# A Fourier-mixing layer and its feed-forward layer in one kernel: the first phase rebuilt

## The chip, the cores and the metric

The kernel runs on one core of a Trainium2 chip. The metric is the device time of one execution in microseconds (us); lower is better. A core has five engines with queues of their own: PE (TensorE, matrix products; its weight loads are shown as PEld), DVE (VectorE), ACT (ScalarE), POOL (GpSimd) and SP (SyncE, which here only issues transfers). Transfers run on the core's 16 DMA engines; SP, ACT and POOL can issue them.

## The reference

For 8 batches of 3008 tokens of 256 features, a real Fourier transform along the tokens is mixed by a complex 256 x 256 weight, biased, shrunk towards zero by 0.01 and transformed back. A feed-forward layer with a squared ReLU follows.

```
X = rfft(x, axis=1);  Xr, Xi = X.real, X.imag          # x: (8, 3008, 256)
Yr = Xr @ w_r - Xi @ w_i + b_r
Yi = Xr @ w_i + Xi @ w_r + b_i
Y  = sign(Y) * max(|Y| - 0.01, 0)                      # on Yr and Yi apart
y  = irfft(Yr + 1j * Yi, n=3008, axis=1)               # float32
h  = y.reshape(24064, 256) @ moe_w_in                  # 256 -> 2048
out = (max(h, 0) ** 2) @ moe_w_out                     # 2048 -> 256
```

The feed-forward weights come as 64-bit floats (two 32-bit words each).

## The kernel before

**Tiling.** A token index is split as 3008 = 47 x 64, so that the transform takes two stages of matrix products. The host folds the 47 rows into 24 pairs and lays x out as 120 rows (24 pairs x 5) by 13 blocks, each block two planes of 256 numbers a row. Stage one (`Fwd32` for batch 0, `Fwd2` for batch 1, `Fwd` after) adds and subtracts the two planes of a block, multiplies by the constant `am32` and stores the result (`xe`) to an intermediate `s1` in device memory. Stage two of batch 0 is made of 24 units (`Unit32`, one for each pair index g): it reads its rows of `s1` (`ka`), multiplies by a constant of its own (`kbb`: `fwd`), copies the spectrum to SBUF (`kx`: `bins`), multiplies by the mix weights (`w32`: `mix`), adds the bias and shrinks (`kv`: `shrink`), multiplies back (`kk`: `back`) and stores the result to `s3` as a high half (`kuh`) and a low half (`kul`), both in fp32r, a 32-bit format that PE multiplies in one pass where float32 takes two (`store_back`). The other batches do the same in pairs (`Pair`) with fp32r products.

**Phases.** The first phase (its own memory pool, `FRONT` gives the number of buffers for each name) does stage one of batch 0, all its units, and the first seven blocks (`PRE`) of stage one of batch 1. `ring` holds the seven `Fwd32` (two blocks each but the last); four of their x buffers (`big`) exist. Between the units stand the conversions of the feed-forward weights: 16 parts of 512 KB (`moe_part`, loaded into `dst`) are turned from 64-bit floats into fp32r halves by `convert` (`bits`, `join`, then `split` or, for w_in, `win_sums`), mostly DVE work. Two parts are converted ahead of the units, eight between them, two straight after, and four later. The seven blocks of batch 1 (`second[q].run`) are multiplied after the last unit, with the sum and difference made by PE (`am32`, `nam`, its negative), copied by ACT to an `xf` buffer, of which there are three, and stored over POOL's queue.

The main loop then walks over 48 tiles of 8 steps (`Step`): the second half of the way back (`Back`, reading `s3` into `du`, copied by ACT as `dy`), the split of the tokens into halves (`Tokens`), and the feed-forward products (`psh`, `pso`), with the remaining stage-one blocks and the pairs of the next batches hung between the steps at written times (`jobs`). Weight parts 13, 14 and 15 are converted at slots 1, 3 and 5 (`LATER`).

**Order.** A tile framework orders each engine's queue by program order and a simulated time line. `tc.issue_after(x)` puts what follows behind x on its queue; every queue runs strictly in order, so a waiting instruction holds all behind it. Buffers of one name are used in turn: a new one waits until the last reader of the old one, a transfer too, has ended.

In the unit loop, round r issues `fwd` and `bins` of unit r + 1, `shrink` of r - 1, `back` and `store` of r - 2 and `mix` of r. PE thus sees forward product, back product, mix product. `store_back` has two ways to the low half: for units 0 to 21 ACT writes a second copy `ku` of the product, and POOL subtracts (22 times); for the last two DVE subtracts straight from PSUM. PSUM has eight banks of 2 KB a partition; the first phase uses six (`psf`).

## Time and profile before

| what | us |
|---|---|
| median of three runs | 2613.54 (2612.62 to 2613.75) |
| span of the profiled execution, first to last instruction | 2611.6 |
| PE busy | 2565.9 (98%) |
| DVE, ACT, POOL busy | 1788.3, 1672.8, 1658.6 |
| DMA moved | 250.51 MB, mean 96 GB/s |
| first product of a unit starts | 34.40 |
| last unit's back product starts | 109.75 |

The profile is that of one execution; its own time is its span and what lies around it, and the span is 1.9 us under the median of the runs. A row of instructions reads: start in us, length, engine, line of the code, operation, what it writes and reads, shapes, and in brackets how long the engine stood idle before it and what ended that. A row of a group gives the count, the busy time, the mean of one in ns, and the idle time before. A row of waits reads: who waited for whom, us in total, times, the longest. A row of transfers gives the queue, the count, KB of one and the median us from issue to landing. On PE one float32 product is two instructions, and a busy PE isn't PE at its peak. Lengths overlap by somewhat less than 0.1 us on DVE and ACT, so the distance between starts is the better measure in a full queue.

### The profile page before, as it was taken

The page shows a single profiled execution, that of the slowest core. Times are in us where ns is not written, and L with a number is a line of the kernel's source. Part 1 is how long each engine was busy: PE and PEld are TensorE (multiplying, and loading weights), DVE is VectorE, ACT ScalarE, POOL GpSimd, SP SyncE. Part 2 cuts the span into 40 slices and gives each one's busy share as a digit, 9 for nine tenths or more (in the row PEclk, how much of TensorE's full clock was granted, in tenths as well). Part 3 has the DMA queues.
Part 4 walks back from the last instruction along what each step waited for, and adds up shares of the span by engine and source line. Part 5 has one row for each costly group of instructions (what it writes and reads, how often), then busy time and mean ns, then how long its engine had stood idle before and what let it go on. Part 6 is the DMA issues. An engine that isn't in the chain of part 4 may idle for free.

```text
span 2611.6 us, 47553 instructions
## 1 busy us (share of the span) xinstructions
PE 2565.9 (98%) x16908; PEld 2347.7 (90%) x16908; DVE 1788.3 (68%) x3797; ACT 1672.8 (64%) x2434; POOL 1658.6 (64%) x1635
## 2 busy tenths in 40 slices
PE   6899999999999999999999999999999999999999
PEld 4789989999999999999999999999999999999998
DVE  7787766667767767577676776667676677765554
ACT  3566656666666666666666666666666666666665
POOL 2256666666766667667666676666667666666564
PEclk8999999999999999999999999999999999999999
DMA  8733332333332333233332333323332223221100
GB/s 265 253 100 106 102 113 80 96 108 104 94 94 78 113 104 88 82 95 114 103 92 82 97 110 100 100 76 100 104 106 82 69 81 101 72 65 40 34 17 17
DMA packets 191070, 250.51 MB, mean 96 GB/s; under 512 B 21790, under 2 KB 135958, under 8 KB 190834
## 3 DMA queue, kind: packets, MB, share of 16 engines
q1 hardware_dynamic: 177970, 223.40, 28.1%
q0 software_dynamic: 12864, 24.07, 3.9%
q8 instruction: 136, 2.23, 0.4%
q14 instruction: 100, 0.82, 0.1%
HBM read 146.85 MB, written 100.53 MB: 95 GB/s over the span
## 4 chain that ended last, share of the span: by engine, by line
PE 93%; DVE 3%; DMA 2%; POOL 1%; issue 1%; ACT 0%; SPq 0%; POOLq 0%; ACTq 0%; DVEq 0%
PE pso L484 39%; PE psh L484 35%; PE psf L301 7%; PE psf L280 3%; PE psf L236 2%; PE psf L333 2%; PE psf L464 1%; PE psf L465 1%; PE psf L461 1%; DMA du<-s 1%; DMA s<-xe 1%; PE psf L415 1%; PE psf L352 0%; DVE kv L101 0%; PE psf L373 0%
## 5 line engine op out<-in xcount | busy, mean ns | idle before, releaser
L101 POOL TENSOR_TENSOR mg<-mc,mg 128x500 fp32r<-128x500 f32 (+1 forms) x768 | 974.8, 1290 | 594.6 <-ACT mg L97 562.0
L484 PE MATMUL pso<-mg,wout 128*128 128x500 f32 (+1 forms) x4608 | 1176.2, 392 | 1.5 <-ACT mg L97 1.3
L484 PE MATMUL psh<-yt,win 128*128 128x250 f32 (+1 forms) x8064 | 1070.1, 281 | 1.6 <-DVE yr L471 1.0
L484 ACT ACTIVATE mc<-mc 128x1000 f32<-128x1000 f32 (+1 forms) x768 | 802.7, 1045 | 414.7 <-DVE mc L484 405.9
L484 PEld LDWEIGHTS psh<-yt,win 128*128 128x128 f32 x8064 | 1020.5, 189 | 33.9 <-PE psh L484 2.0
L484 PEld LDWEIGHTS pso<-mg,wout 128*128 128x128 f32 x4608 | 818.6, 189 | 130.0 <-POOL mg L101 2.0
L484 DVE TENSOR_TENSOR mc<-psh,mv 128x500 f32<-128x500 f32 (+3 forms) x768 | 419.6, 548 | 432.2 <-PE psh L484 399.7
L97 ACT CAST mg<-mc 128x1000 fp32r<-128x1000 f32 (+1 forms) x384 | 397.0, 1034 | 18.3
L484 DVE TENSOR_TENSOR mv<-psh,mu 128x500 f32<-128x500 f32 (+1 forms) x384 | 260.8, 679 | 55.3 <-PE psh L484 22.4
L301 PE MATMUL psf<-wx,kxh 128*128 128x256 f32 x1008 | 207.2, 282 | 1.6 <-ACT xe L97 0.7
L98 DVE COPY mp<-psh 128x250 f32<-128x250 f32 (+1 forms) x384 | 159.9, 416 | 32.5 <-PE psh L484 8.9
L101 POOL TENSOR_TENSOR ksl<-kv,ksh 128x512 fp32r<-128x512 f32 x84 | 108.7, 1294 | 100.6 <-ACT ksh L97 100.5
L301 PEld LDWEIGHTS psf<-wx,kxh 128*128 128x128 f32 x1008 | 166.6, 189 | 6.3 <-ACT xe L97 0.9
L484 DVE TENSOR_TENSOR mu<-psh,mp 128x250 f32<-128x250 f32 (+1 forms) x384 | 160.7, 418 | 11.5
L484 DVE TENSOR_TENSOR mc<-psh,mp 128x250 f32<-128x250 f32 (+1 forms) x384 | 157.1, 409 | 5.8 <-PE psh L484 4.2
L215 POOL TENSOR_TENSOR xs<-xt 120x256 f32<-120x256 f32 x156 | 114.9, 757 | 67.3 <-DMA xt<-x_in 66.6
L322 DVE TENSOR_TENSOR kv<-psf,ke 64x256 f32<-64x256 f32 x336 | 141.8, 422 | 18.1 <-PE psf L301 10.0
L301 PE MATMUL psf<-wx,kxl 128*128 128x256 f32 x504 | 141.5, 281 | 3.6 <-DVE kxl L101 3.6
L97 ACT COPY dy<-psf 128x188 f32<-128x188 f32 x256 | 77.0, 313 | 83.6 <-PE psf L465 82.7
L97 ACT CAST ksh<-kv 128x512 fp32r<-128x512 f32 x84 | 52.1, 620 | 118.0 <-DVE kv L101 117.2
L313 DVE TENSOR_TENSOR ke<-psf,bias 128x512 f32<-128x512 f32 x84 | 58.1, 691 | 100.6 <-PE psf L301 100.2
L97 ACT CAST kuh<-psf 128x256 fp32r<-128x256 f32 x192 | 68.3, 372 | 87.8 <-PE psf L333 72.5
(103 smaller groups left out, 2575.0 us busy)
## 6 DMA issues: line engine op xcount, KB each, us to landing
du<-s SPq DMA_DIRECT2D x128, 256.0 KB, 2.8
s<-kuh SPq DMA_DIRECT2D x192, 128.0 KB, 1.8
s<-kul SPq DMA_DIRECT2D x192, 128.0 KB, 2.0
ka<-s SPq DMA_DIRECT2D x84, 256.0 KB, 3.4
kcm<-cm_in POOLq DMA_DIRECT2D x84, 256.0 KB, 3.3
s<-xe SPq DMA_DIRECT2D x85, 240.0 KB, 2.4
xt<-x_in SPq DMA_DIRECT2D x84, 240.0 KB, 3.4
du<-s SPq DMA_DIRECT2D x256, 64.0 KB, 2.8
```

Source lines behind the costliest of these rows:

```text
L97: return act.copy(out=out, in_=in_)
L98: return eng.tensor_copy(out=out, in_=in_)
L101: return eng.tensor_tensor(out=out, in0=a, in1=b, op=ALU.subtract)
L215: return eng.tensor_tensor(out=out[:, :n], in0=self.xt[:, :n, 0], in1=self.xt[:, :n, 1], op=(ALU.add, ALU.subtract)[t])
L236: nc.tensor.matmul(ps[:M1, t], am32[:, t], self.u[:, t], start=True, stop=True)
L280: nc.tensor.matmul(pv[:, :, c, g, :], self.a[:, g, c * 128:(c + 1) * 128], bg, start=True, stop=True)
L301: self.last = nc.tensor.matmul(ps, l, wx[j][:, k, c, :], start=n == 0, stop=n == 5)
L313: dve.tensor_add(out=self.e, in0=self.pe, in1=bias)
L322: dve.tensor_add(out=v[64 * r:64 * r + 64, g], in0=ps[gs], in1=self.e[gs, r])
L333: nc.tensor.matmul(ps[:, :D], self.cm[:, g, j * 128:(j + 1) * 128], r[:, g], start=n == 0, stop=n == 2)
L415: nc.tensor.matmul(ps[:, :D], self.x[:, c, js], w32[j][:, c], start=n == 0, stop=n == 3)
L484: last_of[eng] = op(*args, **kwargs)
```

## The change

The change touches the first phase only, and what it hands on.

- x is laid out on 128 rows (the last eight are zeros) and `Fwd32` loads all of them. Both folds are made by DVE (one was POOL's), both copies out of PSUM by ACT (one was DVE's).
- The queue of ACT issues `am32`, the mix weights, the bias and the first group of unit constants; the bias arrives as four rows in a block of 34 and is added by one more product in `mix` (fp32r, high and low half against a selector `sel`) in place of DVE's addition of `b32`.
- `shrink` becomes one ReLU on ACT and one DVE operation, min(y + 0.01, relu(y - 0.01)). DVE makes every low half (`kul`) from PSUM; POOL and `ku` drop out of the units.
- Units load two at a time (`ka`, four pairs of buffers in place of five single ones). The constants `kbb` and `kk` of a group of four units are loaded behind the store of unit 3, 7, 11 and 15 (groups 2 to 5); groups 0 and 1 ahead.
- The weight parts are loaded behind the first unit loads (three of them) and then behind the store of every second unit; ten conversions instead of eight stand between the units, none ahead. The bias for the later batches follows unit 2's store.
- Three blocks of batch 1 (`FILL`) are loaded during stage one and multiplied straight after it, seven more (3 to 9) after the last unit, so that `PRE` is 10 instead of 7 and three instead of six are left for the main loop. `xf` has two buffers instead of three, `psf` eight instead of six.

```diff
 FRONT = {
-    "a32": 1, "b32": 1, "w320": 1, "w321": 1, "big": 4, "small": 4, "ds": 1, "dw": 3, "ka": 5, "xe": 7,
-    "kv": 3, "psf": 6, "x6": 7, "xf": 3, "nam": 1,
+    "w320": 1, "w321": 1, "big": 4, "small": 4, "ds": 1, "dw": 3, "ka": 4, "xe": 7, "sel": 1, "bb": 1,
+    "kv": 3, "psf": 8, "x6": 7, "xf": 2, "nam": 1,
 }
...
-    nc.sync.dma_start(am32, a32)
     w32 = []
...
-
     def load_mix_weights():
-        b32 = T("b32", [128, D], F32)
-        for j, v in enumerate((b_r, b_i)):
-            with tc.issue_after(ring[3].folds[1].ins):
-                pool.dma_start(b32[64 * j:64 * j + 64, :], v.unsqueeze(0).broadcast_to([64, D]))
         for j, w in enumerate((w_r, w_i)):
...
             w32.append(st)
-            nc.sync.dma_start(st, w.rearrange("(c p) d -> p c d", p=128))
+            act.dma_start(st, w.rearrange("(c p) d -> p c d", p=128))
+
+    def split_mix_weights():
         wd = T("wd", [128, 2, D], F32, tag="small")
...
             sub(dve, wx[1][:, j], w, wx[0][:, j])
-        return b32
+
+    def load_bias():
+        bf = T("bf", [34, D], F32, tag="small")
+        sf = T("sf", [34, 128], F32, tag="small")
+        act.dma_start(bf, b2)
+        act.dma_start(sf, sel)
+        bb = T("bb", [34, D], F32R)
+        one = T("sel", [34, 128], F32R)
+        copy(act, one, sf)
+        copy(act, bb, bf)
+        sub(dve, bb[32:], bf[32:], bb[32:])
+        return one, bb
...
-        def join(self):
+        def join(self, after=None):
             self.w = w = T("dw", [128, 512], F32)
-            dve.scalar_tensor_tensor(
-                out=w, in0=self.st[:, :, 0].bitcast(U32), scalar=2.0 ** -52, in1=self.a,
-                op0=ALU.mult, op1=ALU.mult,
-            )
+            with tc.issue_after(after.cut.ins) if after else nullcontext():
+                dve.scalar_tensor_tensor(
+                    out=w, in0=self.st[:, :, 0].bitcast(U32), scalar=2.0 ** -52, in1=self.a,
+                    op0=ALU.mult, op1=ALU.mult,
+                )
             dve.tensor_add(out=w, in0=w, in1=self.f.bitcast(F32))
...
         for v, m in ((uh, 4 * g), (ul, 128 + 4 * g if 4 * g < 64 else 32 + 4 * g)):
-            nc.sync.dma_start(rows[m * NP:m * NP + 128], v.bitcast(F32))
-        return done
+            put = nc.sync.dma_start(rows[m * NP:m * NP + 128], v.bitcast(F32))
+        return done, put
...
         def load(self):
-            self.xt = T("x4", [M1, 2, 2, D], F32, tag="big")
+            self.xt = T("x4", [128, 2, 2, D], F32, tag="big")
             self.get = nc.sync.dma_start(self.xt[:, :self.n], x[self.b, :, self.q:self.q + self.n])
...
             n = self.n
-            self.ps, self.folds = [], []
-            for t, eng in enumerate((dve, pool)):
+            self.ps = []
+            for t in range(2):
                 u = T("x2", [M1, 2, D], F32, tag="small")
-                self.folds.append(self.fold(eng, u, t))
+                self.cut = dve.tensor_tensor(
+                    out=u[:, :n], in0=self.xt[:M1, :n, 0], in1=self.xt[:M1, :n, 1], op=(ALU.add, ALU.subtract)[t]
+                )
                 ps = bank([128, 2, D])
...
         def put(self):
+            n = self.n
             self.ev = T("xe", [M1, 2, 2, D], F32)
             for t, ps in enumerate(self.ps):
-                self.done = copy((act, dve)[t], self.ev[:, :self.n, t], ps[:M1, :self.n])
+                self.done = copy(act, self.ev[:, :n, t], ps[:M1, :n])
             self.last = self.store()
...
-    kk = [None, None]
+    group = {}
+
+    def load_group(k, after, eng=nc.sync):
+        group[k] = []
+        for name, src in (("kbb", bm), ("kk", c32)):
+            t = T(name, [128, 4, 128], F32)
+            with tc.issue_after(after.ins):
+                after = eng.dma_start(t, src[:, 4 * k:4 * k + 4])
+            group[k].append(t)
+        return after
...
         def load(self):
-            self.a = T("ka", [128, D], F32)
-            self.get = nc.sync.dma_start(self.a, s1[self.b][self.g, :N1].rearrange("n t c -> (n t) c"))
-            if self.g % 4 == 0:
-                with tc.issue_after(units[self.g - 4].get.ins if self.g else ring[2].last.ins):
-                    for j, (name, src) in enumerate((("kbb", bm), ("kk", c32))):
-                        kk[j] = T(name, [128, 4, 128], F32)
-                        nc.sync.dma_start(kk[j], src[:, self.g:self.g + 4])
-            self.m, self.k = kk[0][:, self.g % 4], kk[1][:, self.g % 4]
+            if self.g % 2 == 0:
+                self.pair = T("ka", [128, 2, D], F32)
+                self.get = nc.sync.dma_start(
+                    self.pair, s1[self.b][self.g:self.g + 2, :N1].rearrange("g n t c -> (n t) g c")
+                )
+            else:
+                self.pair = units[self.g - 1].pair
+            self.a = self.pair[:, self.g % 2]
...
                 nc.tensor.matmul(
-                    ps[:, c, 0:128], self.a[:, c * 128:(c + 1) * 128], self.m, start=True, stop=True
+                    ps[:, c, 0:128], self.a[:, c * 128:(c + 1) * 128], group[self.g // 4][0][:, self.g % 4], start=True, stop=True
                 )
...
             self.ps = ps = bank([128, 512])
+            nc.tensor.matmul(ps[:, :D], one, bb, start=True, stop=False)
             for n in range(4):
...
                 js = slice(64, 192) if j == 0 else slice(0, 128)
-                nc.tensor.matmul(ps[:, :D], self.x[:, c, js], w32[j][:, c], start=n == 0, stop=n == 3)
+                nc.tensor.matmul(ps[:, :D], self.x[:, c, js], w32[j][:, c], start=False, stop=n == 3)
...
             self.v = v = T("kv", [128, D], F32)
-            cl = T("kc", [128, D], F32)
-            dve.tensor_add(out=v, in0=self.ps[:, :D], in1=b32)
-            dve.tensor_scalar(out=cl, in0=v, scalar1=-LAM, scalar2=LAM, op0=ALU.max, op1=ALU.min)
-            self.cut = sub(dve, v, v, cl)
+            r = T("kr", [128, D], F32)
+            act.activation(r, self.ps[:, :D], AF.Relu, bias=low)
+            self.cut = dve.scalar_tensor_tensor(
+                out=v, in0=self.ps[:, :D], scalar=LAM, in1=r, op0=ALU.add, op1=ALU.min
+            )
...
             self.ps = ps = bank([128, 512])
-            nc.tensor.matmul(ps[:, :D], self.k, self.v, start=True, stop=True)
+            nc.tensor.matmul(ps[:, :D], group[self.g // 4][1][:, self.g % 4], self.v, start=True, stop=True)
...
         def store(self):
-            self.done = store_back(self.b, self.g, self.ps[:, :D], pool if self.g < G - 2 else None)
+            self.done, self.put = store_back(self.b, self.g, self.ps[:, :D], None)
...
     parts = [moe_part(q) for q in (0, 1, 8, 9, 2, 3, 10, 11, 4, 5, 12, 13, 6, 7, 14, 15)]
-
+    PRE, FILL = 10, 3
+    second = [Fwd2(1, q) for q in range(J)]
+
+    act.dma_start(am32, a32)
+    dve.memset(low, -LAM)
     for f in ring[:FRONT["big"]]:
         f.load()
+    nam = T("nam", [M1, M1], F32)
+    act.mul(nam, am32[:, 1], -1.0)
+    one, bb = load_bias()
     for r in range(len(ring) + 1):
...
         at(ring, r - 1, "put")
-    with tc.issue_after(ring[2].last.ins):
-        b32 = load_mix_weights()
-
-
-    EARLY, LATE = 2, 6
+        if r == 1:
+            with tc.issue_after(ring[0].done.ins):
+                load_mix_weights()
+                load_group(0, ring[0].done, act)
+        if r == 4:
+            for q in range(FILL):
+                second[q].load_early(ring[2].last)
+    for q in range(FILL):
+        second[q].run()
+    for u in units[:4]:
+        u.load()
+    last = load_group(1, units[0].get)
+    with tc.issue_after(ring[-1].done.ins), tc.issue_after(ring[-1].cut.ins):
+        split_mix_weights()
+
+    AHEAD, LATE = 3, 6
     LATER = {1: 13, 3: 14, 5: 15}
...
-    def convert(n, after=None):
+    def convert(n, after=None, then=None):
         p = parts[n]
         p.bits(after)
-        p.join()
+        p.join(then)
         if n % 4 > 1:
...
-    last = ring[1].last
-    for p in parts[:EARLY]:
+    for p in parts[:AHEAD]:
         with tc.issue_after(last.ins):
...
         last = p.get
-    for n in range(EARLY):
-        convert(n)
-    paced = [(n, 2 * (n - EARLY)) for n in range(EARLY, len(parts) - LATE)]
-    loads = [(k - 1, parts[n]) for n, k in paced] + [(20 + j, p) for j, p in enumerate(parts[-LATE:-2])]
-
-    PRE = 7
-    nam = T("nam", [M1, M1], F32)
-    act.mul(nam, am32[:, 1], -1.0)
-    second = [Fwd2(1, q) for q in range(J)]
-    for r in range(-5, len(units) + 3):
+    loads = parts[AHEAD:-2]
+    for r in range(-1, len(units) + 3):
         at(units, r + 5, "load")
...
         at(units, r, "mix")
-        if r == 4:
-            with tc.issue_after(units[8].get.ins):
-                for j, v in enumerate((b_r, b_i)):
-                    nc.sync.dma_start(bias[:, j, :], v.unsqueeze(0).broadcast_to([128, D]))
-                last_pool = pool.dma_start(dx_sb, dx)
-        while loads and loads[0][0] <= r:
-            p = loads.pop(0)[1]
-            with tc.issue_after((units[r + 5] if r + 5 < len(units) else units[-1]).get.ins):
-                p.load()
-        for n, k in paced:
-            if k + 3 == r:
-                convert(n, units[k])
-        if 0 <= r - 12 < PRE:
-            second[r - 12].load_early(units[min(r + 5, len(units) - 1)].get)
-    for q in range(PRE):
+        k = r - 2
+        if k == 2:
+            with tc.issue_after(units[k].put.ins):
+                for j in range(2):
+                    nc.sync.dma_start(bias[:, j, :], b2[j:j + 1].broadcast_to([128, D]))
+            last_pool = pool.dma_start(dx_sb, dx)
+        if k >= 3 and k % 4 == 3 and k // 4 + 2 < G // 4:
+            load_group(k // 4 + 2, units[k].put)
+        n, odd = divmod(k, 2)
+        if k >= 0 and not odd and n < len(parts) - LATE:
+            convert(n, units[k], units[k])
+            if loads:
+                with tc.issue_after(units[k].put.ins):
+                    loads.pop(0).load()
+        if k >= 12 and k - 12 + FILL < PRE:
+            second[k - 12 + FILL].load_early(units[k].put)
+    for p in loads:
+        with tc.issue_after(units[-1].put.ins):
+            p.load()
+    for q in range(FILL, PRE):
         second[q].run()
-    chain[nc.sync], chain[pool] = units[-1].get, last_pool
+    chain[nc.sync], chain[pool] = units[-1].put, last_pool
     front.close()
...
     xp = xp.reshape(B, N2, R, J, D)
-    xi = np.zeros((B, G, R, J, 2, D), x.dtype)
-    xi[:, :, :, :, 0] = xp[:, :G]
-    xi[:, 1:, :, :, 1] = xp[:, :G - 1:-1]
+    xi = np.zeros((B, 128, J, 2, D), x.dtype)
+    xv = xi[:, :M1].reshape(B, G, R, J, 2, D)
+    xv[:, :, :, :, 0] = xp[:, :G]
+    xv[:, 1:, :, :, 1] = xp[:, :G - 1:-1]
+    xi[:, :M1] = xv.reshape(B, M1, J, 2, D)
     am, bm, cm, dm = _consts()
+    b2, sel = np.zeros((34, D), x.dtype), np.zeros((34, 128), x.dtype)
+    for j, v in enumerate((b_r, b_i)):
+        b2[j] = b2[32 + j] = v
+        sel[j::32, 64 * j:64 * j + 64] = 1
     arrays = {
-        "x_in": xi.reshape(B, M1, J, 2, D),
-        "w_r_in": w_r, "w_i_in": w_i, "b_r_in": b_r, "b_i_in": b_i,
+        "x_in": xi,
+        "w_r_in": w_r, "w_i_in": w_i, "b2_in": b2,
         "w_in_in": moe_w_in.view(np.int64), "w_out_in": moe_w_out.view(np.int64),
...
         "c32_in": cm.transpose(1, 0, 2).astype(np.float32),
+        "sel_in": sel,
     }
```

## Prediction before the run

> **What bounds the kernel now.** I read the page's head, then a table of the span cut at the seams of the stages (columns: stretch in us, its length, busy time of PE, PEld, DVE, ACT and POOL with instruction counts, granted clock, DMA share, GB/s).
>
> ```profile
> span 2611.6 us, 47553 instructions
> 0.00:34.40 34.40, 14.72 (x29) 6.01 (x29) 19.64 (x33) 8.97 (x15) 11.89 (x14) 0.89 0.86 268
> 34.40:110.26 75.86, 68.69 (x337) 59.73 (x337) 67.18 (x146) 39.42 (x113) 20.66 (x22) 0.96 0.84 259
> 110.26:139.06 28.80, 24.82 (x118) 20.99 (x117) 19.20 (x46) 13.09 (x28) 4.08 (x8) 0.88 0.67 212
> 139.06:170.00 30.94, 29.33 (x184) 26.27 (x183) 30.58 (x59) 20.90 (x31) 14.27 (x12) 1.00 0.39 111
> 170.00:2611.60 2441.60, 2428.31 (x16247) 2234.70 (x16245) 1651.69 (x3519) 1590.44 (x2248) 1607.68 (x1580) 1.00 0.30 87
> ```
>
> From 170 us on PE is busy 2428.3 of 2441.6 us and the change moves nothing there. The prize lies in the first 139 us: stage one with its loads (0 to 34.4), the 24 units (34.4 to 110.3), seven blocks of the second batch and the way into the main loop (110.3 to 139.1). Behind these, 139 to 170 is odd: DVE is busy 30.58 of 30.94 us, PE 29.33, so both are full.
>
> How the first stretch ends, by the chain that ended last (start, length, what) and the DMA columns of 1 us windows:
>
> ```profile
> 1.27 4.89 DMA x<-x_in
> 6.18 0.70 DVE x L215
> 6.93 9.34 PE psf L373 x14
> 24.57 7.54 DMA s<-xe
> 32.25 2.05 DMA ka<-s
> 34.40 2.04 PE psf L401 x8
> ...
> 10.00:11.00 1.00, 1.00 (x2) 0.32 (x1) 0.01 (x1) 0.00 (x0) 0.71 (x1) 1.00 0.96 238
> 17.00:18.00 1.00, 1.00 (x4) 0.50 (x3) 1.00 (x1) 0.00 (x0) 1.00 (x2) 1.00 1.01 391
> 24.00:25.00 1.00, 0.00 (x0) 0.00 (x0) 0.00 (x0) 0.48 (x1) 0.00 (x0) 1.00 1.03 415
> 30.00:31.00 1.00, 0.00 (x0) 0.00 (x0) 1.00 (x3) 0.00 (x0) 0.00 (x0) 0.50 0.32 125
> ```
>
> The unit loads wait for the last store of stage one. It is issued at 24.57 and needs 7.54 us because the queue ahead of it holds weights; DMA moves 415 GB/s then and falls off only at 30. While nothing but x, on 120 rows, is in flight (10 to 11) the share is as full, 0.96, at 238 GB/s; with 128-row weights mixed in it is 391.
>
> **The change part by part.**
>
> *Stage one.* x comes as 6.5 loads of 128 x 4 KB (0.524 MB; 3.41 MB in all, before 3.12). I take 390 GB/s from the 17 to 18 row, since that is what 128-row traffic reaches; the other bound is the 238 of the 10 to 11 row. At 390 the first block needs 1.35 us instead of 2, am32 and dx_sb no longer go ahead of it, and it is issued about 0.5 us sooner: PE starts near 5.0 instead of 6.93. Both folds on DVE cost 2 x 0.7 a block, less than PE needs for it. PE's pitch sets the rest (weight loads of one stream, start and length):
>
> ```profile
> 10.49 0.32 PEld L373 LDWEIGHTS psf<-x,am 120*120 120x120 f32 x1 [0.53 <-issue]
> 11.35 0.32 PEld L373 LDWEIGHTS psf<-x,am 120*120 120x120 f32 x1 [0.53 <-issue]
> ...
> 13.52 0.18 PEld L373 LDWEIGHTS psf<-x,am 120*120 120x120 f32 x1 [0.24 <-issue]
> 13.95 0.18 PEld L373 LDWEIGHTS psf<-x,am 120*120 120x120 f32 x1 [0.25 <-issue]
> ```
>
> 0.86 us an instruction until about 13, 0.43 after: slow for the first 6.1 us of work. With that kept, two blocks in the slow 6.1 us and then 4.5 at 4 x 0.43, PE ends near 5.0 + 6.1 + 8 = 19 (before 6.93 + 14.72 = 21.65 at the earliest), and the last store is issued near 20. What must be moved ahead of the unit loads: x 3.41, stores 3.12, mix weights and first group 1.05, three blocks of the second batch 0.74, am32 0.12: 8.44 MB, and 0.2 to 0.5 of the POOL queue's stores between. From 1.8 us at 390 GB/s that ends at 1.8 + 8.44/0.39 = 23.5; if the last 1.3 to 1.7 MB, all on 120 rows, go at 240, at 26 or 27. Taking 25.5 and half a us for landing, the unit loads go out at 26 and, with the 2.05 + 0.1 of the chain, PE starts the units at 28.2 instead of 34.4: **-6 us** (bounds -2.5, x at 238; -8). Seven DMA issues and both evictions move to ACT, beside PE's 1.72 us a block; if ACT is late, eight PSUM banks hold four blocks, and behind them PE would wait for it.
>
> A rule that speaks against this: the Trainium skill, "DMA: Bandwidth & Descriptors", section "Why a DMA increments its semaphore by 16 and not by 1", says a transfer runs on the largest number of engines up to 16 that divides its row counts. By it 120 rows use 15 engines and 128 use 16, which would be only a sixteenth more rate, an estimate of 254 GB/s, and as x also has a fifteenth more bytes, no gain. The row at 17 to 18 speaks for more, but it is a mixture; so this is a rival below.
>
> *The units.* DVE loses the add, clip and subtract and gains one two-input operation and POOL's low half; POOL is idle. Groups of DVE from 43 to 98 us (busy us, mean ns), and DVE's own low half:
>
> ```profile
> L101 DVE TENSOR_TENSOR kv<-kv,kc 128x256 f32<-128x256 f32 x18 | 9.6, 532 | 0.0
> L420 DVE TENSOR_TENSOR kv<-psf,b 128x256 f32<-128x256 f32 x18 | 7.4, 413 | 1.0 <-PE psf L415 1.0
> L421 DVE TENSOR_SCALAR kc<-kv 128x256 f32<-128x256 f32 x18 | 6.7, 372 | 0.1
> 109.91 0.42 DVE L101 TENSOR_TENSOR kul<-psf,kuh 128x256 fp32r<-128x256 f32 x1 [0.30 <-issue]
> ```
>
> 1.32 us a unit becomes 2 x 0.42 = 0.84, 24 x 0.48 = 11.5 us of DVE. But two more conversions come in from the wait before the units. The stage's DVE time without the 24 x 1.32 of the units is 67.18 - 31.7 = 35.5 for eight of them, 4.4 each; so DVE keeps 67.2 - 11.5 + 8.9 = 65 us, and PE becomes the bound. PE's own pace, where DVE had slack:
>
> ```profile
> 101.70 1.89 PE L415 MATMUL psf<-w,kx 128*128 128x256 f32 x8
> 103.43 0.61 PE L401 MATMUL psf<-kbb,ka 128*128 128x128 f32 x4
> 103.87 0.60 PE L426 MATMUL psf<-kv,kk 128*128 128x256 f32 x2
> 104.31 1.89 PE L415 MATMUL psf<-w,kx 128*128 128x256 f32 x8
> ...
> 139.06 2.62 PE L484 MATMUL psh<-yt,win 128*128 128x252 f32 x21
> ```
>
> 104.31 - 101.70 = 2.61 a unit, and the bias product is one more of the 0.12 kind (2.62/21): 2.73. Then 24 x 2.73 = 65.5, plus 3 for the slow clock at the start, 2 for the first unit's chain and 1.5 for the last: 72 us at best against 75.86. Two new waits eat into it:
>
> ```profile
> POOL kul L101 <- DMA s<-kul: 26.3, 8, 4.5
> ...
> s<-kul SPq DMA_DIRECT2D x24, 128.0 KB, 3.9
> kbb<-bm_in SPq DMA_DIRECT2D x4, 256.0 KB, 3.6
> ...
> 109.75 0.67 PE L426 MATMUL psf<-kv,kk 128*128 128x256 f32 x2 [0.97 <-DVE kv L101]
> 111.40 0.38 SPq L255 DMA_DIRECT2D s<-kul  x1
> ```
>
> First, a group of constants is now issued only after the store of unit 3, 7, 11 or 15 and needed by the forward product two units on. Back product to its store's issue is 111.40 - 109.75 = 1.65, with busy engines about 2.1; 0.4 to issue, 3.6 to land: 6.1, against PE's two units less one forward product, 2 x 2.73 - 0.44 = 5.0. PE stalls about 1.1, four times: 4 us if DVE and ACT use none of it, 0 if a load is quicker. Second, POOL waited eight times for one of the two low-half buffers; the same wait now stands in DVE's queue, ahead of the next shrink, which PE's back product awaits. A store of 3.9 us fits into two units (5.5), one of the longer ones does not; I take 1. ACT's relu replaces its plain copy and costs nothing while ACT has half its time free. I put the stage at 74.4: **-1.5 us** (bounds -4 and +12, below).
>
> *The seven later blocks.* As many as before, but through two output buffers instead of three.
>
> ```profile
> ACT xe L97 <- DMA s<-xe: 5.7, 3, 2.0
> s<-xe POOLq DMA_DIRECT2D x7, 240.0 KB, 5.3
> ...
> 123.98 0.59 ACT L97 COPY xe<-psf 120x512 f32<-120x512 f32 x1 [2.02 <-DMA s<-xe]
> 124.67 0.53 ACT L97 COPY dy<-psf 128x188 f32<-128x188 f32 x2
> ```
>
> ACT already waits 5.7 us for the buffers and the first dy copy stands behind the last block. With two, a copy and its store, 0.6 + 0.3 + 5.3, pass two blocks: 3.1 us a block against 1.73 of PE, up to 5 x 1.37 = 7 us more before dy. Part is idle time that another wait would fill, since the first full step of the main loop starts only at 139, and dy copies may be ordered between: **+2.5 us** (0 to +7). One weight part more goes out just before the du loads (0.5 MB, 1.3 us), inside this.
>
> *The main loop.* Three blocks fewer.
>
> ```profile
> 141.52 1.46 PE L352 MATMUL psf<-xt,am 120*120 120x256 f32 x6
> 142.82 0.59 PE L352 MATMUL psf<-xt,nam 120*120 120x256 f32 x2
> ```
>
> 143.25 - 141.52 = 1.73 us of PE each (the next block starts at 143.25), 5.2 for three. They run instead while PE waits for stage one's stores, from about 19 to 24, which costs nothing there as long as they end before 28. In the main loop the two blocks that come first stand where PE waits anyway, and the others in the stretch where DVE is full (30.58 of 30.94): a shorter PE queue there waits for DVE. So of the 5.2 I count **-2 us** (0 to -5.2).
>
> Sum: -6 - 1.5 + 2.5 - 2 = -7. The span of the profiled execution, 2611.6, becomes 2604.6; the median of the runs, 2613.54, lies 1.9 above that span, for what stands around it. Forecast: **2606.5 us**.
>
> **The rivals.**
>
> *All of it lands (2598 us).* Units at PE's pace (-4), DVE with slack while it converts so that all three blocks count (-5.2), the tail's two buffers covered (0): -6 - 4 - 5.2 = -15.2. For it: PE ran at 2.61 a unit when it could. Against: DVE's full stretch behind 139.
>
> *x is not faster (2610).* If 128 rows move x at the 238 GB/s that 120 rows reach, it takes 3.41/0.238 = 14.3 us instead of 8.7, and PE waits for blocks. The stage's gain falls from 6 to 2.5, the sum to -3.5. For it: the DMA share is as full at 238 as at 391. Against: both rows are of the same core and the same kind of load. The rule of the Trainium skill's page above comes near to this case; that 15 of 16 engines would give 238 beside 391 it does not explain.
>
> *The tail takes it back (2614.5).* Two buffers cost the full 7, the units gain nothing (0), DVE eats the three blocks (0): -6 + 7 = +1. It is the buffers' landing that decides, from 5 us on.
>
> *The low half's wait stops DVE (2620.5), the slower one.* If the 26.3 us that POOL waited move to DVE whole, DVE has 65 + 26 = 91 us, less some 3 that the missing POOL no longer stretches (the subtract's 532 ns beside 413): 88, and the stage becomes 12 longer than 75.86: -6 + 12 + 2.5 - 2 = +6.5. For it: eight of 22 stores were late for two buffers, and weights now stand straight behind every second store. Against: POOL was itself held by ACT and stood in a chain with SP, and DVE's low half comes earlier. It decides once most stores take longer than two units, 5.5 us, to land.
>
> **How the numbers follow.** My forecast 0.40, all lands 0.22, x not faster 0.15, the tail 0.13, DVE stopped 0.10. A measurement of this kernel tells about 0.2%, 5.2 us, from no change: faster is below 2608.3, slower above 2618.7. The forecast's own terms spread by 4 us or so, so 0.29 of its 0.40 counts as faster, 0.11 as the same; all lands is faster whole; of x not faster 0.03 is faster; the tail is the same, 0.01 of it slower; DVE stopped is slower by 0.09. Faster 0.54, same 0.36, slower 0.10. The range leaves out the lower part of the second case and most of the last: 2596 to 2616.
>
> **What would show it.** Right: the x-only windows at 350 GB/s or more; unit loads issued by 27; first unit product by 29; back products 2.7 to 3.1 us apart, with short waits of PE for kbb at units 8, 12, 16, 20; DVE's waits for the kul stores a few us in all; ACT's waits for the output buffers 10 us or more ahead of the first dy; in the main loop three blocks fewer and PE with more gaps between its first steps. Wrong: x at 240 to 260 GB/s; last store of stage one landing after 30; the distance from the first unit product to the last back product over 80 us, or under 71; the first steps of the main loop full again more than 10 us earlier, or later, than 139 us. The forecast also fails if the new order moves a stall inside the main loop, which I took as unchanged.

## The result, and the profile after

The changed kernel took 2629.50 us in the median of three runs (2623.79 to 2630.95; a fourth, at 13598.11, lay far above all others and is left out), beside 2613.64 for the kernel before, run together with it: a ratio of 1.0057 (1.0041 to 1.0073). It is slower by 0.57%, where 2606.5 was forecast, and lies outside the range of 2596 to 2616. Its profiled execution has a span of 2629.2 us (time 2630.95), 17.6 more than the 2611.6 of before.

The span of the changed kernel, cut at five events: the first product of a unit, the last back product, the first full step of the main loop (the first `psh` group of 15 or more products), the first outputs of a tile (ACT's first `mo`), the end. Columns as in the prediction's first table. Behind it the two rows of the kernel before that the prediction's table cuts elsewhere.

```profile
0.00:33.89 33.89, 21.86 (x52) 10.99 (x53) 12.02 (x21) 12.77 (x24) 2.52 (x8) 0.95 0.83 282
33.89:116.79 82.90, 78.71 (x358) 60.44 (x358) 60.06 (x132) 43.56 (x118) 0.00 (x0) 0.96 0.78 245
116.79:147.72 30.93, 23.09 (x97) 19.04 (x97) 15.65 (x38) 11.73 (x25) 4.06 (x8) 0.83 0.59 188
147.72:215.39 67.67, 58.33 (x371) 52.85 (x372) 58.00 (x106) 41.07 (x59) 39.87 (x36) 0.92 0.26 75
215.39:2629.20 2413.81, 2401.01 (x16056) 2208.93 (x16054) 1631.59 (x3478) 1570.11 (x2221) 1584.12 (x1556) 1.00 0.29 87
```

```profile
134.49:198.50 64.01, 61.02 (x392) 54.92 (x391) 54.07 (x107) 42.62 (x62) 36.81 (x36) 1.00 0.36 101
198.50:2611.60 2413.10, 2400.15 (x16064) 2209.17 (x16062) 1632.56 (x3478) 1570.02 (x2221) 1585.14 (x1556) 1.00 0.30 87
```

The last row is the same in both within 0.7 us: all that changed lies before the first tile outputs. The same cut for every kernel of this study (lengths of the stretches; runs are told of below):

| kernel | first unit product | units | to first full step | to first tile outputs | rest | span |
|---|---|---|---|---|---|---|
| before | 34.40 | 75.35 | 24.74 | 64.01 | 2413.1 | 2611.6 |
| after | 33.89 | 82.90 | 30.93 | 67.67 | 2413.8 | 2629.2 |
| e1_bias128 | 32.56 | 78.61 | 30.6 | 68.0 | 2409.7 | 2619.5 |
| e2_biasf32 | 32.10 | 82.75 | 31.6 | 66.9 | 2414.3 | 2627.7 |
| e3_xf3 | 32.61 | 82.83 | 31.9 | 68.4 | 2412.4 | 2628.1 |
| e4_biaslate | 31.14 | 85.18 | 31.7 | 67.8 | 2413.7 | 2629.5 |
| e5_kbbearly | 32.12 | 76.69 | 31.0 | 68.9 | 2415.0 | 2623.6 |
| e6_nofill | 30.66 | 81.22 | 31.3 | 64.6 | 2413.3 | 2621.0 |
| e8_later | 33.20 | 82.79 | 31.0 | 60.0 | 2422.0 | 2629.0 |
| e9_pre7 | 32.23 | 81.58 | 22.5 | 64.4 | 2415.8 | 2616.5 |
| c1 | 31.25 | 69.97 | 22.5 | 64.2 | 2413.7 | 2601.6 |
| c4 | 28.02 | 67.48 | 24.8 | 64.9 | 2412.7 | 2597.9 |

After less before, with the forecast's term: start -0.5 (-6), units +7.6 (-1.5), to the first full step +6.2 (+2.5), to the first tile +3.7 (-2), rest +0.7. Six kernels whose stage one is as the change has it, but for the shape or format of the bias block (e1, e2, e3, e5, e8, e9), start between 32.1 and 33.2, so the start varies by 1 us or more from run to run, and a fair term for it is -0.5 to -2.3. Each row is one execution; e1's is that of its fastest run (2621.26 us, median 2626.65).

### The profile page after: what moved, and what is told of

Same layout as the page of the kernel before. It is cut to its first block, busy times and chain, and to the rows that moved or that the text cites. A ratio compares the mean times of both kernels' runs of the same rounds, so it can differ in the third digit from the quotient of the medians.

```text
span 2629.2 us, 47506 instructions
## 1 busy us (share of the span) xinstructions
PE 2583.0 (98%) x16932; PEld 2352.2 (89%) x16932; DVE 1777.3 (68%) x3773; ACT 1679.2 (64%) x2445; POOL 1630.6 (62%) x1607
## 4 chain that ended last, share of the span: by engine, by line
PE 93%; DMA 3%; DVE 2%; POOL 1%; issue 1%; ACT 0%; SPq 0%; ACTq 0%; POOLq 0%; DVEq 0%
PE pso L507 39%; PE psh L507 35%; PE psf L310 7%; PE psf L289 3%; PE psf L245 2%; PE psf L342 2%; PE psf L437 1%; PE psf L487 1%; PE psf L488 1%; PE psf L484 1%; DMA du<-s 1%; DMA s<-xe 1%; DMA kbb<-bm_in 1%; PE psf L422 0%; DMA sf<-sel_in 0%
## 5 line engine op out<-in xcount | busy, mean ns | idle before, releaser
L494 DVE TENSOR_TENSOR yr<-psf,dy 128x188 f32<-128x188 f32 (+4 forms) x256 | 78.2, 313 | 68.1 <-ACT dy L98 61.6
```

What stands on the lines that cost most here:

```text
L494: self.cut = dve.tensor_add(out=o, in0=ps[:, 0, lo:hi], in1=y[:, c, lo:hi])
```

## The experiments

Two theories of the loss were set against each other first: that the units got longer because the bias product costs much more than its size says (A), or because loads come too late for them (B: `kbb`, or a stop of DVE behind the low half's stores); then the start, the way into the main loop and the main loop were tried one at a time. The time of each kernel is a median, and the ratio behind it is to the kernel before, run together with it. By these ratios e1 to e5 and e8 can't be told from the changed kernel: their intervals overlap its 1.0041 to 1.0073. Only e6, e9, c1 and c4 lie below it. What is said of the others rests on the stretches of one execution each.

### e1 and e2: the shape of the bias product

One unit of the changed kernel in PE's timeline (start, length, line, operation, count):

```profile
64.32 1.99 PE L437 MATMUL psf<-w,kx 128*128 128x256 f32 x8
66.15 0.61 PE L422 MATMUL psf<-kbb,ka 128*128 128x128 f32 x4
66.59 0.60 PE L449 MATMUL psf<-kv,kk 128*128 128x256 f32 x2
67.12 0.38 PE L433 MATMUL psf<-bb,sel 34*128 34x256 f32 x1
67.43 1.99 PE L437 MATMUL psf<-w,kx 128*128 128x256 f32 x8
```

67.43 - 64.32 = 3.11 us a unit, where before it was 2.61. The new row itself takes 67.43 - 67.12 = 0.31, the back product ahead of it 0.53 (0.44 before), and the mix behind it 1.83 instead of 1.73. PE's weight loads show the seam:

```profile
66.48 0.30 PEld L449 LDWEIGHTS psf<-kv,kk 128*128 128x128 f32 x2
67.12 0.18 PEld L433 LDWEIGHTS psf<-bb,sel 34*128 34x128 f32 x1 [0.33 <-issue]
67.43 1.59 PEld L437 LDWEIGHTS psf<-w,kx 128*128 128x128 f32 x8
```

The load of the 34-row weights starts at 67.12, with its product and not under the one before it; the unit's own loads (66.48) run ahead of their products (66.59). e1 puts the same bias into 128 rows, 94 of them zero; e2 keeps 34 rows and makes them plain float32.

```diff
-        bb = T("bb", [34, D], F32R)
-        one = T("sel", [34, 128], F32R)
-        copy(act, one, sf)
-        copy(act, bb, bf)
+        bb = T("bb", [128, D], F32R)             # e1; e2: [34, ...] in F32
+        one = T("sel", [128, 128], F32R)
+        pool.memset(bb.bitcast(F32), 0.0)        # and one
+        copy(act, one[:34], sf)
+        copy(act, bb[:34], bf)
...
```

> The changed kernel with one edit: the bias product has 128 rows (34 as before, the rest zeros) instead of 34, still fp32r; nothing else. In the changed kernel a unit takes PE 3.11 us from mix product to mix product: bias 0.31, mix 1.92, forward 0.44, back 0.43, where the mix took 1.73 before. Theory A, the 34-row shape is what PE pays for when it stands between 128-row products: bias falls to about 0.12 and mix to 1.73, a unit to about 2.73, 24 units 9 us shorter unless DVE or the waits for kbb take it back. Theory B, PE pays for each change between fp32r and float32: the unit stays at 3.1 us.

> The changed kernel with one edit: the bias product keeps its 34 rows but is float32 (two passes). Theory B (change of format): bias 0.43 and mix back to 1.73, a unit about 3.03 us, 2 us less over 24. Theory A (shape of 34 rows): the mix keeps its 1.92, the bias takes about 0.6, a unit about 3.4, 7 us more over 24.

e1: 2626.65 us, a ratio of 1.0053 (1.0035 to 1.0070) to before. A unit of it, in the same view:

```profile
56.36 0.60 PE L451 MATMUL psf<-kv,kk 128*128 128x256 f32 x2
56.60 0.47 PE L435 MATMUL psf<-bb,sel 128*128 128x256 f32 x1
56.91 1.89 PE L439 MATMUL psf<-w,kx 128*128 128x256 f32 x8
58.63 0.61 PE L424 MATMUL psf<-kbb,ka 128*128 128x128 f32 x4
59.08 0.60 PE L451 MATMUL psf<-kv,kk 128*128 128x256 f32 x2
```

59.08 - 56.36 = 2.72 us a unit, 0.39 less with more rows to multiply: 9.4 us over 24 units. e2 (2630.03 us, 1.0073, 1.0056 to 1.0090) has 3.43 a unit, 0.32 more than after, for a second instruction of the same shape (0.70 for the two). Its 24 units still take 82.75 us and not 7 more: no wait for `kbb` is left in them, and the granted clock was 1.00 from their start. So it is the shape between products of 128 rows that costs, and not a change between fp32r and float32: theory A. The Trainium skill, "TensorEngine Tiling (Array Packing)", section "Tiling Modes", says that a change of the array's tiling mode drains TensorE, and that there are modes of 64 and of 32 rows. The weight load that no longer overlaps and the two stretched neighbours fit that; no row shows the mode itself.

Of the 9.4 us only 4.3 came through in e1's units (78.61). And 2.1 of the 4.3 lie ahead of the first back product (7.32 us beside 9.47), where the granted clock was at 0.50 for 3.4 us in e1 and for 6.8 in the changed kernel, which the edit doesn't reach. Behind it PE's busy time falls by 6.9 us (62.37 beside 69.24), but PE, now ahead, waits 4.6 longer for `kbb`, so that 2.1 are left (waits of PE over the units, in us, times, longest; the changed kernel first, then e1):

```profile
PE psf L422 <- DMA kbb<-bm_in: 3.5, 3, 1.5
```

```profile
PE psf L424 <- DMA kbb<-bm_in: 8.1, 4, 3.5
```

### e5: the constants earlier

```diff
...
-        if k >= 3 and k % 4 == 3 and k // 4 + 2 < G // 4:
-            load_group(k // 4 + 2, units[k].put)
+        if k >= 3 and k % 4 == 3 and k // 4 + 2 < G // 4:
+            load_group(k // 4 + 2, units[k].put, names=("kk",))
+        if k >= 1 and k % 4 == 1 and k // 4 + 2 < G // 4:
+            load_group(k // 4 + 2, units[k].put, names=("kbb",))
```

> The changed kernel with one edit: a group's forward constants kbb are loaded behind the store of units 1, 5, 9, 13 instead of 3, 7, 11, 15 (their buffer is free from then); kk stays. In the changed kernel PE waits for kbb before units 8, 16 and 20, 1.1, 1.0 and 1.5 us by the profile and 3.9 us by the starts of its products. Theory: the waits go and the 24 units take 79 us instead of 82.9. Rival: the wait is lent time, DVE and the stores catch up in it, and PE waits elsewhere; the stage stays over 82.

2625.66 us, 1.0052 (1.0036 to 1.0068). No wait for `kbb` is left. The units take 76.69 instead of 82.90, of which two stretches (first product to first back product, then to the last) show what is the edit's, after first and e5 second:

```profile
33.89:43.36 9.47, 9.47 (x34) 7.55 (x35) 0.52 (x2) 1.96 (x7) 0.00 (x0) 0.64 0.98 343
43.36:116.79 73.43, 69.24 (x325) 52.88 (x324) 59.54 (x131) 41.60 (x111) 0.00 (x0) 1.00 0.75 233
```

```profile
32.12:38.46 6.34, 6.34 (x35) 5.27 (x35) 0.42 (x1) 2.13 (x8) 0.53 (x1) 1.00 0.97 286
38.46:108.81 70.35, 68.51 (x325) 53.19 (x324) 59.73 (x131) 41.58 (x111) 0.00 (x0) 1.00 0.84 264
```

3.1 us lie behind the first back product, which is about the wait of 3.5; the other 3.1 lie before it, where PE's granted clock was 0.64 in the one execution and 1.00 in the other. The edit doesn't reach that stretch, so that half is not its gain, and the edit's own is close to the 79 us expected (82.90 - 3.1 = 79.8). What set the clock there isn't settled; PE had stood idle 2.16 us before its first unit product in the one and 0.46 in the other.

### e4 and e6: the start

The load of the selector in the chain of the changed kernel (start, length), ACT's queue, and four windows of 1 us (the last column GB/s):

```profile
1.70 9.83 DMA sf<-sel_in
...
9.44 0.40 ACT L98 CAST bb<-bf 34x256 fp32r<-34x256 f32 x1 [4.06 <-DMA bf<-b_in]
9.75 0.57 ACT L98 COPY xe<-psf 120x512 f32<-120x512 f32 x1
11.56 0.30 ACT L98 CAST sel<-sf 34x128 fp32r<-34x128 f32 x1 [1.24 <-DMA sf<-sel_in]
11.76 0.57 ACT L98 COPY xe<-psf 120x512 f32<-120x512 f32 x1
...
8.00:9.00 1.00, 1.00 (x2) 0.28 (x1) 0.40 (x1) 0.00 (x0) 0.00 (x0) 1.00 1.08 372
10.00:11.00 1.00, 1.00 (x2) 0.00 (x0) 0.97 (x2) 0.32 (x1) 0.00 (x0) 1.00 0.21 69
11.00:12.00 1.00, 1.00 (x3) 0.28 (x2) 0.12 (x2) 0.44 (x2) 0.00 (x0) 1.00 0.11 20
12.00:13.00 1.00, 0.55 (x2) 0.28 (x2) 1.00 (x2) 0.34 (x1) 0.00 (x0) 1.00 0.81 156
```

x on 128 rows does run fast: 367 to 406 GB/s from 3 to 10 us, 372 in the row shown, where 120 rows gave 238. But ACT, which now makes both copies out of PSUM and issues the first weights, waits for two loads of 34 rows that share the DMA engines with x; the one for `sel` is the longest piece in the chain of waits of this stretch, 9.83 us from its start at 1.70. The copies and loads behind it came late, the last x load only at 13.21, and the DMA engines ran nearly empty from 10 to 12 (69 and 20 GB/s). e4 gives the two a buffer of their own and casts them after stage one; e6 leaves out the three early blocks (none in stage one, seven behind the units, six in the main loop, as before).

```diff
+        bf = T("bf", [34, D], F32)               # e4: no longer tag="small"
+        sf = T("sf", [34, 128], F32)
...
     with tc.issue_after(ring[-1].done.ins), tc.issue_after(ring[-1].cut.ins):
+        one, bb = cast_bias(bf, sf)
         split_mix_weights()
```
```diff
-    PRE, FILL = 10, 3
+    PRE, FILL = 7, 0                             # e6
```

> The changed kernel with one edit: the two small bias loads have buffers of their own and ACT casts them after stage one instead of ahead of the first copies out of PSUM. In the changed kernel ACT stands until 11.56 for them, the first store and the last x load behind it on SP are issued at 12.4 and 13.2, DMA is idle from 10 to 12.9, and the units start at 33.9. Theory: this wait is what ate the gain of stage one; the last x load lands by 16 instead of 20.5, the unit loads are issued near 27.5 instead of 30.5, the units start near 31, 3 us less in all. Rival: transfers by volume bound the stage; the unit loads go out after 29.5 all the same.

> No block of the second batch in stage one, seven behind the units, six in the main loop, as in the kernel before; the rest as in the changed kernel. Theory F (what lengthens the way from the first full step to the first tile outputs is having only three blocks in the main loop): that way is 64.4 us instead of 67.7, and PE's 7.3 us wait in step 3 is gone, though the seven blocks behind the units stay (31 us from the last back product to the first full step). Theory T (the late first full step, 31 us instead of 24.7 behind the units, is what pushes the conversions into step 3): the wait of about 7 us stays, the way is 67 us or longer. The three blocks in stage one cost its loads 0.74 MB: without them the first unit product comes about 1 to 2 us earlier than 33.9. By F the span is 2629.2 - 1.5 - 3.3 + up to 2 for the rest = 2624 to 2627, by T 2628 to 2632.

e4: 2632.20 us, 1.0071 (1.0055 to 1.0086). The hole is gone (365 to 380 GB/s from 10 to 13), the unit loads go out at 28.24 instead of 30.54, and the first unit product comes at 31.14, as its theory had it. That is 1 to 2.8 us earlier than with the wait, and still 2.9 later than the 28.2 of the forecast: the stage is then bound by its volume, 9.0 MB between 2 and 28 us at a mean of 345 GB/s. The windows from 19 to 23 give only 266 to 309, while stores and the last loads, both of 120 rows, are in flight. In c4, whose windows from 19 to 23 hold almost nothing but such stores, they give 352 to 381, so 120 rows alone are not the reason, and no run here names it. The gain of the start didn't reach the end: the 85.18 us of e4's units hold a clock of 0.50 from 30.8 to 37.7 us and two waits for `kbb` of 1.8 and 2.1; the late cast is not among PE's waits.

e6: 2620.33 us, 1.0029 (1.0018 to 1.0040), 9 us under the changed kernel, and its span of 2621.0 is under both expectations. The start is 1.4 to 3.2 us earlier than in the kernels with the three blocks in stage one; 0.74 MB at 0.345 MB/us would be 2.1. And the stretch into the first tile is 64.6 again: theory F of its expectation. It is taken up below.

### e3: a third output buffer

The tail behind the last unit: ACT waits for the two `xf` buffers, and PE's first product of the way back stands behind ACT (waits from 110 to 150 us; us, times, longest):

```profile
ACT xe L98 <- DMA s<-xe: 8.6, 4, 4.9
PE psf L484 <- ACT xe L98: 6.2, 1, 6.2
```

```diff
-    "kv": 3, "psf": 8, "x6": 7, "xf": 2, "nam": 1,
+    "kv": 3, "psf": 8, "x6": 7, "xf": 3, "nam": 1,
```

> The changed kernel with one edit: three output buffers xf for the early blocks instead of two, as before. In the changed kernel it is 19.0 us from the last back product to the first product of the way back (12.4 before), 6.2 of them PE waiting for ACT's copy. Theory: the two buffers cost this; it falls to 12.5 to 14 us, and the kernel gets 5 us shorter. Rival: the stores' landing is slow because of the transfers around them and ACT waits anyway, 17 us or more; or the time comes back as a wait later in the way into the main loop, so that the first full step comes no earlier.

2630.66 us, 1.0069 (1.0054 to 1.0084): nothing gained. PE's rows with a wait in e3:

```profile
131.31 0.33 PE L484 MATMUL psf<-dx_sb,du 128*128 128x188 f32 x1 [3.08 <-DMA du<-s]
133.65 0.71 PE L488 MATMUL psf<-dx_sb,du 128*128 128x188 f32 x2 [1.67 <-DMA du<-s]
141.88 2.89 PE L361 MATMUL psf<-xt,am 120*120 120x256 f32 x6 [2.31 <-DMA xt<-x_in]
```

The first product of the way back comes 15.9 us after the last back product instead of 19.0, but the first full step no earlier (31.9 us beside 30.9). The wait for ACT turns into waits of 3.08, 1.67 and 2.31 for loads: the first `du` load goes out only at 128.26, where the changed kernel's went out at 120.54, because SP's queue waits for PE's blocks ahead of it:

```profile
SPq L109 <- PE psf L361: 9.0, 1, 9.0
```

Probably `du` now lies in memory that these blocks still read; no row shows that. So the edit moved the loads too, and e3 doesn't isolate what the two buffers cost. That they cost something with seven blocks behind the units is seen beside it: the kernel before, with seven blocks and three buffers, takes 24.74 us from the last back product to the first full step; e6, with seven and two, takes 31.3, and PE waits 7.4 for ACT in it. With four blocks and two buffers it takes 22.5 (e9, below).

### e9, e8 and e6: the main loop's first steps

The 3.7 us lost before the first tile outputs stand in one place of the changed kernel, PE first, then DVE's queue up to it:

```profile
168.99 0.95 PE L507 MATMUL psh<-yt,win 128*128 128x252 f32 x6 [1.04 <-DVE mu L507]
177.24 1.62 PE L507 MATMUL psh<-yt,win 128*128 128x252 f32 x6 [7.30 <-DVE mc L507]
...
171.12 1.41 DVE L168 SCALAR_TENSOR_TENSOR dw<-dst,da 128x512 f32<-128x512 uint32 x1
172.45 0.67 DVE L507 TENSOR_TENSOR mv<-psh,mu 128x504 f32<-128x504 f32 x1
173.04 0.41 DVE L159 TENSOR_SCALAR da<-da 128x512 f32<-128x512 f32 x1
173.38 1.73 DVE L172 TENSOR_TENSOR dw<-dw,df 128x512 f32<-128x512 f32 x1
175.03 1.73 DVE L102 TENSOR_TENSOR win<-ds,win 128x1024 fp32r<-128x1024 f32 x1
176.69 1.00 DVE L507 TENSOR_TENSOR mc<-psh,mv 128x252 f32<-128x252 f32 x2
```

Between `mv` and `mc` of one step stand three pieces of three weight conversions (parts 15, 14 and 13), 176.69 - 173.04 = 3.65 us, and ahead of `mv` one more (L168 at 171.12). PE, with three blocks fewer to do meanwhile, waits 7.30 us. e9 makes four blocks behind the units instead of seven, so six in the main loop; e8 keeps seven and three but puts the conversions of parts 14 and 15 two and four slots later.

```diff
-    PRE, FILL = 10, 3
+    PRE, FILL = 7, 3                             # e9
...
-    LATER = {1: 13, 3: 14, 5: 15}
+    LATER = {1: 13, 5: 14, 9: 15}                # e8
```

> The changed kernel with one edit: the three early blocks count against the seven that follow the units, not against the main loop: four blocks after the last unit (7 in the changed kernel), six in the main loop as before. Theory: behind the units ACT copies four blocks through two buffers instead of seven, so the first product of the way back comes 8 to 10 us after the last back product instead of 19, the first full step 22 instead of 31, and since the main loop's start is held by DVE the three more blocks cost little there; the kernel is 6 to 9 us shorter than the changed one. Rival: the way into the main loop is bound by its loads, not by the blocks, and the three blocks cost their 5.2 us in the main loop: no shorter.

> The changed kernel with one edit: the last three weight parts are converted at slots 1, 5 and 9 of the main loop instead of 1, 3 and 5. In the changed kernel PE stands 7.3 us for DVE at 177 (before: nothing that long), and from the first full step to the first tile's output it takes 67.7 us against 64.0 before, though two blocks fewer stand in it. Theory: DVE is full there, with the conversions written into its queue between a step's operations; spread out, the stall goes, the distance falls to 60 to 62, and the kernel is 6 us shorter. Rival: DVE has the same work whenever it is done, the distance stays above 66.

e9: 2618.40 us, 1.0025 (1.0015 to 1.0035), 11 us under the changed kernel, more than the 6 to 9 expected. From the last back product to the first full step it needs 22.5 us instead of 30.9, 2.8 us less for each of three blocks; and though those three now stand in the main loop with 5.2 us of PE's work, the way to the first tile gets shorter, 64.4 instead of 67.7. e6, whose seven blocks behind the units keep the 31.3 us, has that as well. The row of e6 that stands where the changed kernel waited 7.30:

```profile
170.45 0.94 PE L507 MATMUL psh<-yt,win 128*128 128x252 f32 x6 [0.85 <-DVE mc L507]
```

So it is not the late first full step that makes the wait but the missing blocks: DVE's queue has no gap from 155 to 186 us, and blocks taken out of PE's queue leave a wait in their place.

That alone would leave the way as long as it was; it got longer because DVE's work in it did. In the stretches above DVE is busy for 58.00 us with 106 instructions in the changed kernel, for 54.07 with 107 before, and in e6 for 53.90 with 108. The conversions' pieces are the longer ones: `dw<-dw,df` takes 1.73 us at 173.38 above and 0.68 in e6 (e6's stretch, then such a piece):

```profile
143.15:207.71 64.56, 61.30 (x392) 55.04 (x391) 53.90 (x108) 42.38 (x62) 36.53 (x36) 1.00 0.35 101
166.45 0.68 DVE L172 TENSOR_TENSOR dw<-dw,df 128x512 f32<-128x512 f32 x1
```

POOL is busy throughout the 1.73 us and idle throughout the 0.68. Most of the long pieces stand beside a busy POOL, though not every piece beside it is long, and no run varied POOL's work alone, so that this makes them long is likely but not shown. PE's granted clock was also at 0.50 from 171.4 to 181.6, behind its own wait; what that adds isn't separated.

e8: 2631.50 us, 1.0075 (1.0052 to 1.0097). The wait is gone and the first tile is reached in 60.0 us, 7.7 sooner, but the second tile takes 66.2 where the changed kernel's takes 53.7:

```profile
146.98:206.99 60.01, 53.82 (x346) 47.90 (x345) 54.20 (x98) 38.64 (x51) 38.19 (x32) 1.00 0.26 75
206.99:273.21 66.22, 60.85 (x405) 55.87 (x404) 46.74 (x96) 37.43 (x58) 37.17 (x40) 0.95 0.33 99
```

DVE's conversions have moved there with their cost. Written later, DVE's work made its wait later.

### c1 and c4: the parts put together

c1 takes e1, e4, e5 and e9 at once (the x buffers of the early blocks, `x6`, go from seven to six to make room). c4 is c1 without early blocks in stage one and with nine in the main loop.

```diff
-    PRE, FILL = 7, 3                             # c1
+    PRE, FILL = 4, 0                             # c4
```

> The changed kernel with four edits together: the bias product on 128 rows, the bias casts after stage one, kbb loaded two units earlier, and the three early blocks taken from the seven behind the units (with six x6 buffers). By the single terms: units start at 31 (before 34.4), take 24 x 2.72 + 7 = 72 us (before 75.4), the first full step 22 us after the last back product (before 24.7): first full step near 126 against 134.5, and from there the main loop as in the kernel before if its stall of 7.3 us does not return, 8 us under it, or 1 us under it if the stall returns. Rival: DVE becomes the bound of the units at this pace, the stage stays near 78, and the kernel ends level with the one before or above it.

> As c1 (bias product on 128 rows, bias casts late, kbb two units earlier, six blocks in the main loop), but no block of the second batch in stage one, four behind the units and nine in the main loop. Theory V (stage one ends when its volume is through): 0.74 MB less and c1's three blocks of PE work gone, so that the first unit product comes 2.5 to 3.5 us earlier than in c1 (28 to 29 instead of 31.25); units and tail as in c1 (70 and 22.5). Theory D (DVE sets the early main loop, so blocks there are nearly free for PE): the way from the first full step to the first tile outputs stays at 64 to 65 us, the span 2598 to 2600. Theory P (PE sets it, a block costs its 1.73 us): the way is 64.2 + 5.2 = 69.4 us and the span 2603 to 2605.

c1: 2606.57 us, 0.9979 (0.9968 to 0.9990) of before, 6 us by the medians and 10 by the spans, where 8 was expected if the stall stayed away. It did (no wait of PE over 1.0 us between the first full step and the first tile), and DVE is not the bound of the units, which take 69.97 us. c4: 2600.80 us, 0.9954 (0.9941 to 0.9968): 12.6 us under the kernel before, 29 under the changed one. c4's stretches, as in the first table:

```profile
0.00:28.02 28.02, 13.91 (x28) 5.96 (x29) 12.64 (x21) 10.97 (x21) 1.36 (x7) 0.94 0.85 305
28.02:95.50 67.48, 66.71 (x358) 60.07 (x358) 58.30 (x132) 43.60 (x118) 0.00 (x0) 0.98 0.89 284
95.50:120.31 24.81, 18.91 (x71) 15.15 (x72) 17.05 (x40) 10.27 (x23) 2.51 (x5) 0.72 0.66 209
120.31:185.20 64.89, 64.49 (x408) 58.41 (x407) 50.05 (x100) 42.50 (x60) 32.56 (x30) 1.00 0.41 118
```

Stage one without the small waits and without the early blocks starts the units at 28.02, 3.2 us before c1 (theory V); the units run at PE's pace (66.71 of 67.48 busy). Nine blocks in the main loop leave the way to the first tile at 64.9 us, 0.7 more than with six (theory D), though 2.3 us more went into the stretch before it: three blocks there cost 3.0 us in all, where PE's time for them is 5.2, and three blocks in stage one cost 3.2. Against c1 these two would be even; what c4 gains beyond them is in the units (67.48 beside 69.97). Of these 2.5 us 1.1 lie ahead of the first back product, where the granted clock is at 0.50 for 5.4 us in c1 and for 3.3 in c4: 2.1 us at half the clock, which is the 1.1. For the rest no run here names the cause. The spans differ by 3.7 us; the medians, of runs made apart, by 5.8.

## Why the prediction was wrong

The largest error is the term of the units, -1.5 forecast and +7.6 measured, and the step that failed in it is the price of the bias product: "one more of the 0.12 kind (2.62/21)". That row is of products of 128 rows; this one has 34. It costs 0.50 a unit: 0.11 as any product, which e1 confirms (2.72 where 2.73 was worked out), and 0.39 for its shape (e1, e2). 24 x 0.39 = 9.4 added to the forecast's 74.4 makes 83.8; measured, up to the first block behind the units, where the 74.4 ends too (117.33), were 83.4. The other steps of the term held nearly: the waits for `kbb`, "about 1.1, four times: 4 us", came three times, at 1.09, 0.99 and 1.45, and DVE was busy for 60.06 us where 65 was worked out, so that PE was the bound. The low half's wait, the rival with the slower end, didn't happen: DVE shows no wait for a store of `kul` in any kernel of this study. The kernel ended 9.0 us above that rival's 2620.5 (its own terms, +6.5, give 2620.0), by another mechanism.

The second is the start, -6 forecast, -0.5 to -2.3 measured. What failed is a wait that the prediction did not have, and the rate at which the volume moves. The unit loads went out at 30.54 and the first product came at 33.89, where 27 and 29 were to show it right. x itself ran at 367 to 406 GB/s, so the rival "x is not faster" falls. The Trainium skill, "DMA: Bandwidth & Descriptors", section "Why a DMA increments its semaphore by 16 and not by 1", by which 16 engines instead of 15 made an estimate of 254, does not tell this difference; the measurement decides. But "if ACT is late" was written down as a matter of PSUM banks, and what stood in ACT's queue ahead of its first copies, two casts that wait for two small loads, was passed over: 1 to 2.8 us (e4). The volume was right, 8.44 MB and 0.2 to 0.5 of POOL's stores beside 9.0 in e4, but it was to be through at 25.5 us, which is 356 to 377 GB/s from 1.8 us on, and e4 needed until 28, at 345. That the end of the stage would be slower was foreseen ("if the last 1.3 to 1.7 MB, all on 120 rows, go at 240, at 26 or 27"), and 25.5 was taken. The early blocks were costed at nothing "as long as they end before 28"; their loads are in the volume, and leaving them out moved the units 1.4 to 3.2 us forward (e6) and 3.2 (c4 beside c1). With both out, c4 starts at 28.02, where the prediction said 28.2 for the change with the blocks in.

The third, seven blocks through two buffers, was right in kind, 6.2 within 0 to 7; mis-sized was the value taken, 2.5, which counted on idle time that would cover the wait. Nothing covered it: PE stood 6.2 us for ACT's copy in front of the way back, and the first full step came 30.9 us after the last back product instead of 24.7. e3, the test of it, moved the loads as well, so how much of the 6.2 is the two buffers' alone stays open.

The fourth, -2 for three blocks fewer in the main loop, became +3.7, outside its bounds. The prediction saw DVE full there (30.58 of 30.94) and said that "a shorter PE queue there waits for DVE", which is what happened. The step that failed is the bound of 0: it took DVE's work as fixed, and that work grew from 54.07 to 58.00 us in the stretch, with conversion pieces in other places of DVE's queue and longer than before. e6 and e9 put the blocks back and get 3.1 and 3.3 us for it. The prediction's last sentence named this case: a stall moved inside the main loop.

## What to carry to other kernels

A small product isn't priced by its size: here an instruction of another shape between products of one shape had its own cost and stretched both neighbours, and padding it with zeros to the common shape was the cheaper way. When work is moved to another engine, read what already stands in that engine's queue, casts of small loads above all, before costing the move at nothing. Where another engine was full, taking work from PE gained nothing, and the place to give PE more of it was that very stretch. An edit of one buffer count can move transfers that have nothing to do with it, so look at their starts before reading the result as the price of the buffer.

## What the hardware showed that was not expected

- A product of 34 rows between products of 128 rows cost 0.39 us more than the same one padded to 128 rows (3.11 beside 2.72 a unit).
- A load of 34 rows, 512 bytes each, that was issued among x loads of 512 KB took 9.83 us to land.
- At the start of the units the granted clock of PE was 0.64 in one kernel and 1.00 in another with the same work there (9.47 and 6.34 us for it). In the twelve traces it was at 0.50 in the first microseconds of the units in the ten kernels in which PE had stood 2.07 us or more before its first unit product, and not in the two in which it had stood 1.71 (e2) and 0.46 (e5). Each is one execution and nothing was varied for it, so what decides it isn't settled.
- The same DVE instruction (`dw<-dw,df`, 128x512) took 0.68 us with POOL idle and 1.73 with POOL busy throughout; no run varied POOL's work alone.
